# Three attention edits in one fused kernel: state reads in three float32r passes, conversions of w_out moved to the third stage, and token chunks of 368, 368 and 352 columns

## The chip, the cores and the metric

The kernel runs on one core of a Trainium2 chip, in one launch. The time is that of the device in microseconds. Three runs of the kernel before gave 825.01, 826.60 and 826.59 us, so the median is 826.59 us. The engines are named as in the profile: PE (TensorE matmul), PEld (its weight loads), DVE (VectorE), ACT (ScalarE), POOL (GpSimd) and SP, which issues the DMAs.

## The reference

The input is `x` of 4 x 8 heads x 512 tokens x 64 and a small `state` of 32 tokens for each head. Attention goes both ways and gives 4 x (512 + 32) = 2176 rows of 512 features, on which two MLPs follow.

```python
scores = scale * x @ state.T;  a = softmax(scores);   xread = a @ state
scores2 = scale * state @ x.T; a2 = softmax(scores2); sread = a2 @ x
x = concat([xread, sread])                  # tokens x 512
h = x @ w_in                                # 512 -> 2048
g = where(h >= 1, h, where(h <= -1, 0, (h + 1) ** 2 / 4))
y = g @ w_out                               # 2048 -> 512
out = ((y @ w_a) * (y @ w_b)) @ w_out2      # 512 -> 1536 -> 512
```

The weights of both MLPs arrive as float64; the kernel turns them into float32 itself. The matmuls of the MLPs are done in float32r: each float32 operand is split into a high part that float32r holds exactly and the rest, and three passes (high x high, high x low, low x high) make one product.

## The kernel before

There are four stages. In the first, attention is worked through in 8 quads (4 heads of one batch each), and at the same time the first product `x @ w_in` runs in tiles of 128 features x one token block; the blocks are 512, 512, 512, 320 and 320 tokens, so there are 80 tiles (`h_mm`, 12 matmuls each). Each tile's `g` is stored to DRAM. In the second stage (`b_chunk`) the product `g @ w_out` is made by a seven-product scheme (Strassen's, in Winograd's form) that halves tokens and features; in the third (`ab_run`) `y @ w_a` and `y @ w_b` are made in the same way. Both of these go over the tokens in three chunks. `CH` gives a chunk's columns and where its two halves start, so one chunk of 362 columns stands for 2 x 362 tokens, and the three together for 2176. The fourth stage (`o_group`) makes the last product.

Names that the change touches. `a_load` fetches a quad's `x` (`xld`) and state (`st`); `a_qk` makes the scores; `a_soft` the softmax down to `at`, the transposed weights; `a_read` reads the state, `st.T @ at`, in two matmuls of plain float32, one for the partitions 0 to 63 and one for 64 to 127, each into a PSUM bank of its own (6 and 7 in turn), and splits the result into the high and low parts of `x`. `s_soft`, `s_tr` and `s_read` are the other direction. `split` makes the two parts of an operand (one ACT and one DVE instruction). `conv` turns float64 words into float32: two loads, one ACT and four DVE instructions. `u_conv` is new. `w_put` and `w_sums` prepare the weights of the third stage in it.

The order of the work is not that of the code. Every operation is recorded with what it reads and writes (`Flow.op`), and `Flow.order` then plays a list schedule: each engine takes the ready operation with the earliest due time, with costs that are written into the code. Only the matmuls that are not `loose` keep the order of the code. The attention matmuls are `loose`, so a change in their costs or dependencies moves instructions on all engines. Each engine then runs its list strictly in order.

Of the kernel before, what the change touches and what calls it, by code (L numbers as in the profile page):

```python
# [20 lines left out]
class Flow:  # L21
# [16 lines left out]
    def op(self, engs, emit, rd=(), wr=(), size=0, loose=False):  # L38
        i = len(self.ops)
        if loose:  # L40
            self.loose.add(i)
        deps = set()
        last, readers = self.last, self.readers

        def cells(regs):
            for space, lo, hi in regs:
                g = self.GRAIN[space[0]]
                for c in range(lo // g, -(-hi // g)):
                    yield space, c
# [12 lines left out]
        self.ops.append((engs, emit, sorted(deps), size))  # L62
        return i
# [97 lines left out]
def attention_then_two_mlps(  # L161
# [13 lines left out]
    nc = tc.nc  # L175
    P = 128
    NQ = xt_d.shape[0]
# [7 lines left out]
    OFF = [sum(BLK[:j]) for j in range(len(BLK))]  # L185
    NB = len(BLK)

    CH = [(362, 0, 362), (362, 724, 1086), (364, 1448, 1812)]
    PAD = 368
    SCALE = 0.125  # L190
    WARM = 11


    QUAD = 8 * PAD * 4
# [28 lines left out]
    class V2:  # L223
# [17 lines left out]
        @property  # L241
        def regs(self):
            a = BASE[self.arena] + self.at
            return [("S", a + 4 * self.step * i, a + 4 * (self.step * i + self.n)) for i in range(self.k)]
# [17 lines left out]
    def bank(b):  # L262
        return ("P", b, b + 1)

    def dram(name, row, a, b):
        return ("D" + name, row * 4096 + a, row * 4096 + b)
# [27 lines left out]
    def store(dst, src, wr, size):  # L294
        op({"SP": 0.06}, lambda e: nc.sync.dma_start(out=dst(), in_=src()), regs(src), wr, size)
# [170 lines left out]
    def a_soft(k):  # L466
        d = qs[k]
        t1, b = d["t1"], sbank[k]
        mx, sm = d["sm"].sub(16, 16), d["sm"].sub(32, 16)
        op({"DVE": 0.72}, lambda e: nc.vector.transpose(t1(), banks[b]), [bank(b)], regs(t1))  # L470
        op({"DVE": 0.69}, lambda e: nc.vector.reduce_max(mx(), g32(t1()), axis=AX.X), regs(t1), regs(mx))
        op(
            {"POOL": 1.35},
            lambda e: eng(e).tensor_tensor(g32(t1()), g32(t1()), b32(mx()), ALU.subtract),
            regs(t1, mx),
            regs(t1),
        )
        act(t1, t1, 512, AF.Exp, regs(t1), regs(t1), scale=SCALE)
        op({"DVE": 0.69}, lambda e: nc.vector.reduce_sum(sm(), g32(t1()), axis=AX.X), regs(t1), regs(sm))
        op({"DVE": 0.25}, lambda e: nc.vector.tensor_scalar(sm(), sm(), 1e-9, None, ALU.add), regs(sm), regs(sm))  # L480
        op({"DVE": 0.25}, lambda e: nc.vector.reciprocal(sm(), sm()), regs(sm), regs(sm))
        op(
            {"POOL": 1.35},
            lambda e: eng(e).tensor_tensor(g32(t1()), g32(t1()), b32(sm()), ALU.mult),
            regs(t1, sm),
            regs(t1),
        )
        op({"DVE": 0.71}, lambda e: nc.vector.transpose(d["at"](), t1()), regs(t1), regs(d["at"]))

    def a_read(k):  # L490
        d = qs[k]
        b, q = divmod(k, 2)
        for p in range(2):
            ab = abank()
            r = slice(64 * p, 64 * p + 64)

            def emit(e, ab=ab, r=r):
                nc.tensor.matmul(banks[ab], d["st"]()[r, 128:], d["at"]()[r, :], start=True, stop=True)  # L498

            op({"PE": 0.9}, emit, regs(d["st"], d["at"]), [bank(ab)], loose=True)  # L500
            m = 2 * q + p
            for j, o, c, n in x_parts(b * S, S):
                hi, lo = (x[j][i].sub(m * BLK[j] + o, n) for i in range(2))
                src = lambda ab=ab, c=c, n=n: banks[ab][:, c : c + n]
                hi_of(hi, src, n, [bank(ab)], regs(hi))
                tt(lo, src, lambda hi=hi: hi(F32), ALU.subtract, n, [bank(ab)] + regs(hi), regs(lo))
# [292 lines left out]
    def x2_chunk(c, at):  # L799
        n, t0, t1 = CH[c]  # L800
        q = [V2(at[0], at[1] + 2944 * i, 2, PAD, n) for i in range(4)]
        for v, (r, tok) in zip(q, ((0, t0), (0, t1), (2, t0), (2, t1))):
            load(
                v,
                lambda r=r, tok=tok: x2_d[r : r + 2, :, tok : tok + n].rearrange("k p n -> p k n"),
                [dram("X", r + i, tok, tok + n) for i in range(2)],
                1024 * n,
            )
        b11, b12, b21, b22 = q

# [12 lines left out]
        v_sum(b21, b21, b22, ALU.subtract)  # L823
        sp("4", b21)
# [161 lines left out]
    def phase_one():  # L986
        a_load(0)
        a_load(1)
        for k in range(2):
            w_in(k, 1)  # L990
            a_qk(k)
            a_soft(k)
        warm(WARM)
        a_read(0)
        a_read(1)
        nv = nw = 0
        for t, (j, f) in enumerate((j, f) for j in range(NB) for f in range(F1)):
            if j == 0 and f % 2 == 0 and f + 2 < F1:
                w_in(f + 2, 2)
            h_mm(j, f)  # L1000

            if t in (0, 2, 8, 12, 17, 21, 25, 29):
                k = (0, 2, 8, 12, 17, 21, 25, 29).index(t)
                s_soft(k)
                s_tr(k)
                s_read(k)
                if k + 2 < NQ:
                    a_load(k + 2)
                    a_qk(k + 2)
                    a_soft(k + 2)  # L1010
                    a_read(k + 2)
            if 28 <= t < 60 and t % 4 == 0:
                conv([w1_d[2 * (nv + i) + 1] for i in range(2)], stage_a(), V("F0", vraw[nv].at, 1024))
                nv += 2
            if 34 <= t < 66 and t % 4 == 2:

                d = w32_a()
                ks = (F2 + nw, F2 + nw + 1) if nw < 4 else (nw - 4, nw - 3)
                conv([w2_d[3 * (k % F2 % 2) + k % F2 // 2 if k >= F2 else 3 * k + 2] for k in ks], stage_a(), d)
                for i, k in enumerate(ks):  # L1020
                    store(lambda k=k: u_d[k], d.sub(512 * i, 512), [dram("U", k, 0, 512)], 1 << 18)
                nw += 2
        assert (nv, nw) == (F1, F2 + 4)

    stage_l = Ring([V("F1", 2 * QUAD - 3584, 2048)])
    stage_c = Ring([V("F0", 11776 + 8192 * i, 2048) for i in range(2)])
# [15 lines left out]
    for c in range(3):  # L1042
        b_chunk(c, late if c == 2 else lambda k: None)
    x2_chunk(2, ("F0", VRAW))
    for fp in range(F2 // 2):
        for c in range(3):
            more = fp + 1 < F2 // 2
            s = 2 * fp + 2

            def done_a(c=c, s=s, more=more):  # L1050
                if c == 2 and more:
                    w_put(s + 1, combs[1 + s % 2])

# [77 lines left out]
```

## Time and profile before

| | before |
|---|---|
| median of 3 runs | 826.59 us (825.01 to 826.60) |
| profiled execution, whole time | 824.32 us |
| profiled execution, span of the instructions | 822.5 us |
| PE busy | 800.4 us (97%) |
| DVE / ACT busy | 570.7 us (69%) / 397.4 us (48%) |
| mean granted TensorE clock | 0.991 |

The span is 1.8 us shorter than the profiled execution's own time; the rest lies around it. The stages by the trace: the first 24 us are a start in which PE mostly waits; the first stage's tiles run to 255 us, the second stage to 423, the third to 679, the fourth to the end. Busy times of PE are made of records whose ends are modelled and which overlap, so the pace of PE is read from the number of matmuls in a stretch, not from its busy share.

### The profile page before, as it was taken

To read this page: it belongs to the slowest core of one execution; us is meant where nothing else is said; L and a number is where in the kernel's file an instruction comes from. 1 tells how busy PE (TensorE), PEld (TensorE's weight loads), DVE (VectorE), ACT (ScalarE), POOL (GpSimd) and SP (SyncE) were. 2 spreads that over 40 slices of the span, in tenths; PEclk is the share of its full clock that TensorE was granted. 3 is DMA by queue.
4 is the path that set the end of the run, shared out by engine and by line. 5 is a ranking of instruction groups with operands and counts; after the bars stand their busy time and mean duration, and the time that the engine had idled before them with its cause. 6 is when DMAs were issued, how large, how long until landed. Compare 5 with 4: busy or idle time off the path is not lost.

```text
span 822.5 us, 11669 instructions
## 1 busy us (share of the span) xinstructions
PE 800.4 (97%) x4338; PEld 727.2 (88%) x4338; DVE 570.7 (69%) x847; ACT 397.4 (48%) x655; POOL 21.6 (3%) x22
## 2 busy tenths in 40 slices
PE   4999999999999999999999999999999999999997
PEld 2766667889999999999999999999999998888886
DVE  6999998888567886886989998858464674322100
ACT  2777657656587444445665444343423563222100
POOL 2001120000000000000000000000000000000000
PEclk8899999999999999999999999999999999999999
DMA  8676686787634671270543344413142466433101
GB/s 300 207 272 213 200 290 242 277 281 260 229 118 136 218 234 50 81 224 19 157 146 109 119 143 154 153 48 134 50 163 71 142 191 215 142 102 100 68 0 65
DMA packets 71865, 130.01 MB, mean 158 GB/s; under 512 B 7168, under 2 KB 41472, under 8 KB 71808
## 3 DMA queue, kind: packets, MB, share of 16 engines
q1 hardware_dynamic: 71808, 129.27, 47.3%
q8 instruction: 34, 0.56, 0.3%
q14 instruction: 23, 0.19, 0.1%
HBM read 84.93 MB, written 44.30 MB: 157 GB/s over the span
## 4 chain that ended last, share of the span: by engine, by line
PE 86%; DVE 8%; DMA 2%; issue 2%; ACT 1%; SPq 1%; DVEq 0%; ACTq 0%
PE bank L328 82%; DMA f<-in_w_dram 2%; PE bank L498 1%; DVE f L379 1%; PE bank L563 1%; DVE f L371 1%; DVE f L313 1%; DVE r L313 1%; DVE f L357 1%; DVE f L612 1%; DMA g_d<-f 1%; ACT f L304 1%; SPq L292 0%; DVE f L363 0%; PE bank L454 0%
## 5 line engine op out<-in xcount | busy, mean ns | idle before, releaser
L328 PE MATMUL bank<-r 128*128 128x512 f32 (+3 forms) x3084 | 596.6, 351 | 3.1 <-DVE r L313 1.6
L328 PEld LDWEIGHTS bank<-r 128*128 128x128 f32 x3084 | 531.1, 188 | 61.5 <-issue 8.6
L313 DVE TENSOR_TENSOR r<-f,r 128x512 fp32r<-128x512 f32 (+5 forms) x224 | 190.8, 864 | 109.3 <-ACT r L304 103.7
L304 ACT ACTIVATE r<-f 128x512 fp32r<-128x512 f32 (+5 forms) x224 | 170.1, 771 | 171.6 <-PE bank L328 154.3
L328 PE MATMUL bank<-r,r 128*128 128x362 f32 (+1 forms) x1008 | 178.4, 329 | 1.6 <-DVE f L313 1.1
L328 PEld LDWEIGHTS bank<-r,r 128*128 128x128 f32 x1008 | 169.1, 189 | 2.8 <-DVE f L313 2.1
L304 ACT ACTIVATE f<-bank 128x362 f32<-128x362 f32 (+2 forms) x167 | 80.5, 485 | 162.6 <-PE bank L328 161.1
L313 DVE TENSOR_TENSOR f<-bank,f 128x362 f32<-128x362 f32 (+1 forms) x144 | 75.6, 532 | 61.2 <-PE bank L328 52.2
L304 ACT ACTIVATE f<-f 128x512 f32<-128x512 f32 (+2 forms) x123 | 87.3, 724 | 25.9 <-DMA f<-in_w_dram 18.7
L313 DVE TENSOR_TENSOR f<-f 128x256 f32<-128x256 f32 (+5 forms) x110 | 83.1, 778 | 0.3
L605 ACT ACTIVATE f<-bank,half 128x512 f32<-128x512 f32 (+1 forms) x80 | 49.4, 622 | 42.7 <-PE bank L328 36.4
L612 DVE SCALAR_TENSOR_TENSOR f<-f,bank 128x512 f32<-128x512 f32 (+1 forms) x80 | 47.4, 602 | 17.9 <-ACT f L304 11.8
L371 DVE SCALAR_TENSOR_TENSOR f<-f 128x1024 uint32<-128x1024 uint32 (+1 forms) x35 | 43.0, 1230 | 0.3
L379 DVE SCALAR_TENSOR_TENSOR f<-f 128x1024 uint32<-128x1024 uint32 (+1 forms) x35 | 42.6, 1218 | 0.1
L357 DVE TENSOR_SCALAR f<-f 128x1024 f32<-128x1024 f32 (+1 forms) x35 | 25.6, 733 | 9.8 <-ACT f L304 9.2
L965 DVE COPY f<-bank 128x512 f32<-128x512 f32 x8 | 5.5, 692 | 28.1 <-PE bank L328 28.1
L498 PE MATMUL bank<-f 64*128 64x512 f32 x32 | 16.1, 765 | 8.9 <-DVE f L480 6.6
L363 DVE TENSOR_SCALAR f<-f 128x1024 uint32<-128x1024 uint32 (+1 forms) x35 | 24.1, 687 | 0.1
L313 DVE TENSOR_TENSOR f<-f,f 128x724 f32<-128x724 f32 (+1 forms) x24 | 21.6, 908 | 0.9 <-DMA f<-g_d 0.8
L304 ACT ACTIVATE r<-bank 64x64 fp32r<-64x64 f32 (+3 forms) x36 | 13.4, 378 | 16.6 <-PE bank L498 7.9
L498 PEld LDWEIGHTS bank<-f 64*128 64x128 f32 x32 | 4.6, 216 | 15.0 <-DVE f L480 7.4
L313 DVE TENSOR_TENSOR r<-bank,r 64x64 fp32r<-64x64 f32 (+3 forms) x36 | 14.6, 413 | 3.3 <-ACT r L304 3.0
(33 smaller groups left out, 130.1 us busy)
## 6 DMA issues: line engine op xcount, KB each, us to landing
f<-in_w_dram SPq DMA_DIRECT2D x68, 512.0 KB, 4.7
g_d<-f SPq DMA_DIRECT2D x48, 256.0 KB, 4.0
f<-p_d SPq DMA_DIRECT2D x48, 256.0 KB, 2.8
f<-g_d SPq DMA_DIRECT2D x32, 362.0 KB, 4.3
p_d<-f SPq DMA_DIRECT2D x48, 181.0 KB, 2.4
f<-g_d SPq DMA_DIRECT2D x16, 364.0 KB, 4.0
g_d<-f SPq DMA_DIRECT2D x32, 160.0 KB, 1.8
p_d<-f SPq DMA_DIRECT2D x24, 182.0 KB, 2.0
```

Of the source, the lines that this page charges most:

```text
L304: lambda e: nc.scalar.activation(dst(), src(), func, **{k: (v() if callable(v) else v) for k, v in kws.items()}),
L313: op({"DVE": t_tt(n)}, lambda e: nc.vector.tensor_tensor(dst(), a(), b(), alu), rd, wr)
L328: nc.tensor.matmul(o, w, x, start=first and k == 0, stop=last and k == n - 1, skip_group_check=onto)
L357: lambda e: nc.vector.tensor_scalar(dst(), dst(), LEAST, MOST, ALU.max, ALU.min),
L363: lambda e: nc.vector.tensor_scalar(dst(U32), dst(U32), 3, 0x3FFFFFFF, ALU.logical_shift_left, ALU.bitwise_and),
L371: lambda e: nc.vector.scalar_tensor_tensor(dst(U32), word(1, U32)(), 0xC0000000, dst(U32), ALU.bitwise_and, ALU.bitwise_or),
L379: lambda e: nc.vector.scalar_tensor_tensor(dst(U32), word(0, U32)(), 29, dst(U32), ALU.logical_shift_right, ALU.bitwise_or),
L498: nc.tensor.matmul(banks[ab], d["st"]()[r, 128:], d["at"]()[r, :], start=True, stop=True)
L563: nc.tensor.matmul(banks[ab][:, p * 64 : (p + 1) * 64], d["xn"]()[:, c * 256 + p * 128 : c * 256 + (p + 1) * 128], d["a2t"]()[:, c * 128 + ...
L605: lambda e: nc.scalar.activation(q(), h(), AF.Relu, bias=half[:, 0:1], scale=0.5),
L612: lambda e: nc.vector.scalar_tensor_tensor(g(), q(), 1.0, h(), ALU.min, ALU.max),
L965: op({"DVE": t_tt(512)}, lambda e, o=o, b=b: nc.vector.tensor_copy(o(), banks[b]), [bank(b)], regs(o))
```

## The change

There are three edits. First, in quads 4 to 7 the state read is made in three float32r passes: the state's 128 columns and `at` are split into two parts each (`s3`, `w3`), and one operation issues six matmuls, the two partition halves alternating, into both banks. Quads 0 to 3 keep the two float32 matmuls. A further branch for the scores (`x3`) is written for quads from 99 on, of which there are none. Second, the third weight matrix of the second MLP (`w_out2`, 12 blocks, `u_d`) was converted in the first stage, two blocks at a time; now it is converted block by block in the third stage (`u_conv`). In the first stage two conversions for the first blocks of `w_a` and `w_b` are left. Third, the chunks have 368, 368 and 352 columns in place of 362, 362 and 364.

```diff
-    CH = [(362, 0, 362), (362, 724, 1086), (364, 1448, 1812)]
+    CH = [(368, 0, 368), (368, 736, 1104), (352, 1472, 1824)]
...
+    for k in range(4, NQ):
+        o = (XAT[4] + 10240, XAT[2] + 16384)[k % 2]
+        qs[k]["w3"] = [V("R0", o + 2048 * i, 512) for i in range(2)]
+        qs[k]["s3"] = [V("R0", o + 4096 + 512 * i, 128) for i in range(2)]
...
     def a_qk(k):
+        if "w3" in d:
+            split(*d["s3"], d["st"].sub(128, 128))
...
         op({"DVE": 0.71}, lambda e: nc.vector.transpose(d["at"](), t1()), regs(t1), regs(d["at"]))
+        if "w3" in d:
+            split(*d["w3"], d["at"])
 
     def a_read(k):
         d = qs[k]
         b, q = divmod(k, 2)
+        abs_ = [abank() for _ in range(2)]
+        if "w3" in d:
+
+            def emit3(e):
+                for i, (w, x) in enumerate(three(d["s3"], d["w3"])):
+                    for p in range(2):
+                        r = slice(64 * p, 64 * p + 64)
+                        nc.tensor.matmul(banks[abs_[p]], w()[r, :], x()[r, :], start=i == 0, stop=i == 2)
+
+            op({"PE": 0.75}, emit3, regs(*d["s3"], *d["w3"]), [bank(ab) for ab in abs_], loose=True)
         for p in range(2):
-            ab = abank()
+            ab = abs_[p]
...
-            op({"PE": 0.9}, emit, regs(d["st"], d["at"]), [bank(ab)], loose=True)
+            if "w3" not in d:
+                op({"PE": 0.9}, emit, regs(d["st"], d["at"]), [bank(ab)], loose=True)
...
-            if 34 <= t < 66 and t % 4 == 2:
+            if t in (62, 66):
 
                 d = w32_a()
-                ks = (F2 + nw, F2 + nw + 1) if nw < 4 else (nw - 4, nw - 3)
-                conv([w2_d[3 * (k % F2 % 2) + k % F2 // 2 if k >= F2 else 3 * k + 2] for k in ks], stage_a(), d)
...
+                conv([w2_d[3 * i + nw // 2] for i in range(2)], stage_a(), d)
...
+    def u_conv():
+
+        k, d = nu[0], V("F0", 36352, 512)
+        conv([w2_d[3 * k + 2]], stage_c(), d)
+        store(lambda: u_d[k], d, [dram("U", k, 0, 512)], 1 << 18)
+        nu[0] += 1
+
     for fp in range(F2 // 2):
         for c in range(3):
...
+            if fp and nu[0] < F2:
+                u_conv()
```

What this does to the order is read at three places. The first is PE's list in the first stage around the read of quad 4 (L498 before; L529 is the new read, L537 the old one in the new file; L454 and L481 are the scores, L328 and L329 the tiles of `h_mm`, L549 and L589 the transposes, L563 and L603 the `s_read`). Before:

```order
L563 MATMUL bank_74<-f_89 128x64 x8
L454 MATMUL bank_72<-f_66 64x512 x2
L328 MATMUL bank_68<-r_65 128x512 x12
L498 MATMUL bank_73<-f_89 128x512
L498 MATMUL bank_74<-f_89 128x512
L328 MATMUL bank_69<-r_65 128x512 x12
```

And now:

```order
L329 MATMUL bank_67<-r_65 128x512 x12
L481 MATMUL bank_72<-f_66 64x512 x2
L603 MATMUL bank_74<-f_89 128x64 x8
L481 MATMUL bank_71<-f_89 64x512 x2
L329 MATMUL bank_68<-r_65 128x512 x12
L529 MATMUL bank_73<-r_65 128x512
L529 MATMUL bank_74<-r_65 128x512
```

The last two rows come three times in a row. The scores of quad 6 (bank_71) now stand before the read of quad 4, where they stood after it, and the scores of quad 5 (bank_72) before the `s_read`.

The second place is SP's list, where the states of quads 4 to 7 are fetched (`in_st`; f_89 is the buffer of even quads, f_66 that of odd ones). Before, each fetch waited for the read of the quad two before it:

```order
L292 DMA f_66<-in_st_dram 128x256
L295 DMA g_d<-f_89 128x512
L292 DMA f_89<-in_xn_dram 128x1024
L295 DMA g_d<-f_89 128x512
L292 DMA f_66<-in_xt_dram 128x512 x2
L292 DMA f_66<-in_w_dram 128x1024 x2
L292 DMA f_89<-in_st_dram 128x256
```

Now quad 6's fetch waits for the split of quad 4's state alone, and stands just ahead of quad 5's:

```order
L293 DMA f_89<-in_st_dram 128x256
L293 DMA f_66<-in_st_dram 128x256
L296 DMA g_d<-f_89 128x512
L293 DMA f_66<-in_xt_dram 128x512 x2
L293 DMA f_66<-in_st_dram 128x256
L296 DMA g_d<-f_89 128x512
```

The fetches of quads 6, 5 and 7 (in this order) are now close together, and the weights' fetch is behind them.

The third place is DVE's list at the end of the first stage, where the tiles become 320 tokens wide (L612 and L652 make `g` and free the tile's bank; L357, L363 and L371 belong to a conversion). Before:

```order
L612 SCALAR_TENSOR_TENSOR f_89<-f_89,bank_69 128x320
L313 TENSOR_TENSOR r_65<-f_89,r_65 128x2x362
L357 TENSOR_SCALAR f_66<-f_66 128x1024
L363 TENSOR_SCALAR f_66<-f_66 128x1024
L371 SCALAR_TENSOR_TENSOR f_66<-f_66 128x1024
L612 SCALAR_TENSOR_TENSOR f_89<-f_66,bank_70 128x320
```

And now:

```order
L652 SCALAR_TENSOR_TENSOR f_89<-f_89,bank_67 128x320
L314 TENSOR_TENSOR r_65<-f_89,r_65 128x736
L652 SCALAR_TENSOR_TENSOR f_89<-f_66,bank_68 128x320
L652 SCALAR_TENSOR_TENSOR f_89<-f_89,bank_69 128x320
L652 SCALAR_TENSOR_TENSOR f_89<-f_66,bank_70 128x320
```

The conversions between the bank releases are gone from there.

## Rows read from the trace of the kernel before

**Rows 1.** Page, part 1: busy us (share of the span) xinstructions.

```profile
PE 800.4 (97%) x4338; PEld 727.2 (88%) x4338; DVE 570.7 (69%) x847; ACT 397.4 (48%) x655; POOL 21.6 (3%) x22
```

**Rows 2.** Busy by stretch: us, PE (x), PEld, DVE, ACT, POOL, clock, DMA, GB/s.

```profile
24.00:200.00 176.00, 173.26 (x805) 132.92 (x804) 158.33 (x245) 120.10 (x198) 16.41 (x12) 0.99 0.73 251
200.00:255.00 55.00, 53.66 (x364) 53.13 (x364) 35.37 (x53) 38.62 (x72) 0.00 (x0) 1.00 0.50 170
255.00:367.00 112.00, 112.00 (x672) 111.61 (x671) 91.12 (x115) 55.62 (x76) 0.00 (x0) 1.00 0.53 163
367.00:423.00 56.00, 56.00 (x337) 55.80 (x336) 45.72 (x56) 32.53 (x46) 0.00 (x0) 1.00 0.31 102
423.00:476.00 53.00, 51.35 (x304) 50.15 (x303) 49.38 (x73) 29.97 (x49) 0.00 (x0) 1.00 0.38 121
476.00:679.00 203.00, 202.25 (x1214) 201.95 (x1213) 142.49 (x225) 84.22 (x153) 0.00 (x0) 1.00 0.37 125
```

**Rows 3.** Waits of PE: who it waited for, us in total, times, longest.

```profile
PE bank L328 <- DVE r L313: 2.1, 3, 0.8
PE bank L549 <- DVE r L313: 1.2, 1, 1.2
PE bank L328 <- DVE f L612: 1.2, 1, 1.2
PE bank L328 <- DVE f L313: 1.1, 2, 0.7
```

**Rows 4.** As rows 2, stretches of one width: 320, 362, 364, 512 columns.

```profile
225.00:250.00 25.00, 25.00 (x171) 25.00 (x172) 17.00 (x25) 21.05 (x39) 0.00 (x0) 1.00 0.34 114
260.00:360.00 100.00, 100.00 (x601) 99.74 (x599) 81.33 (x105) 48.11 (x66) 0.00 (x0) 1.00 0.51 158
370.00:420.00 50.00, 50.00 (x301) 49.80 (x300) 40.71 (x49) 29.59 (x41) 0.00 (x0) 1.00 0.33 107
700.00:800.00 100.00, 100.00 (x443) 82.84 (x442) 21.80 (x39) 20.29 (x39) 0.00 (x0) 1.00 0.27 85
```

**Rows 5.** PE's timeline: start us, us, instructions; reads of quads 4, 6, 7.

```profile
92.17 1.25 PE L498 MATMUL bank<-f 64*128 64x512 f32 x4
...
118.21 1.13 PE L498 MATMUL bank<-f 64*128 64x512 f32 x4
119.27 5.76 PE L328 MATMUL bank<-r 128*128 128x512 f32 x24
...
129.89 1.12 PE L498 MATMUL bank<-f 64*128 64x512 f32 x2
130.95 3.01 PE L328 MATMUL bank<-r 128*128 128x512 f32 x12
133.89 1.12 PE L498 MATMUL bank<-f 64*128 64x512 f32 x2
```

**Rows 6.** Splits of 128x512, 476 to 679 us: busy us, mean ns | idle before.

```profile
L313 DVE TENSOR_TENSOR r<-f,r 128x512 fp32r<-128x512 f32 x35 | 23.0, 683 | 0.0
L304 ACT ACTIVATE r<-f 128x512 fp32r<-128x512 f32 x37 | 21.9, 626 | 5.5 <-PE bank L328 5.2 <-DVE f L379 0.2
```

**Rows 7.** As rows 2, the stretch of the reads of quads 4 to 6.

```profile
84.00:118.00 34.00, 32.63 (x159) 22.86 (x158) 32.02 (x56) 20.63 (x38) 6.89 (x5) 1.00 0.66 230
```

**Rows 8.** DMA issues: KB each, median us to landing.

```profile
f<-in_st_dram SPq DMA_DIRECT2D x8, 128.0 KB, 2.8
```

**Rows 9.** DVE's instructions of a conversion, 24 to 200 us.

```profile
L379 DVE SCALAR_TENSOR_TENSOR f<-f 128x1024 uint32<-128x1024 uint32 x21 | 26.7, 1272 | 0.1
L371 DVE SCALAR_TENSOR_TENSOR f<-f 128x1024 uint32<-128x1024 uint32 x21 | 26.3, 1252 | 0.2
L357 DVE TENSOR_SCALAR f<-f 128x1024 f32<-128x1024 f32 x21 | 16.3, 776 | 6.9 <-ACT f L304 6.5
L363 DVE TENSOR_SCALAR f<-f 128x1024 uint32<-128x1024 uint32 x21 | 14.6, 694 | 0.1
```

**Rows 10.** Timeline around 207 us, the conversion before PE's wait for L612.

```profile
207.32 0.69 DVE L357 TENSOR_SCALAR f<-f 128x1024 f32<-128x1024 f32 x1 [2.72 <-ACT f L304]
```

**Rows 11.** Waits of DVE from 476 to 679 us.

```profile
DVE f L313 <- PE bank L328: 47.5, 53, 2.5
```

More of the change, by code (lines that the diff above doesn't have):

```diff
@@ L191, in attention_then_two_mlps @@
     WARM = 11
+    STEPS = (0, 2, 8, 12, 17, 21, 25, 29)
     QUAD = 8 * PAD * 4
@@ L427, in attention_then_two_mlps @@
     qs = [{**sets[k % 2], "a2": a2s[k % 2], "sm": sms[k % 4]} for k in range(NQ)]
+    for k in range(4, NQ):
+        o = (XAT[4] + 10240, XAT[2] + 16384)[k % 2]
+        qs[k]["w3"] = [V("R0", o + 2048 * i, 512) for i in range(2)]
+        qs[k]["s3"] = [V("R0", o + 4096 + 512 * i, 128) for i in range(2)]
+        if k >= 99:
+            qs[k]["x3"] = [V("R0", XAT[1] + 8192 * (k % 2) + 4096 * i, 1024) for i in range(2)]
+            qs[k]["q3"] = [V("R0", o + 5120 + 512 * i, 128) for i in range(2)]
     sbank = [4 + k % 2 for k in range(NQ)]
@@ L449, in a_qk @@
         b = sbank[k]
+        if "w3" in d:
+            split(*d["s3"], d["st"].sub(128, 128))
+        if "x3" in d:
+            for i in range(2):
+                split(*(v.sub(512 * i, 512) for v in d["x3"]), d["xld"].sub(512 * i, 512))
+            split(*d["q3"], d["st"].sub(0, 128))
+            def emit3(e):
+                for k, (w, x) in enumerate(three(d["q3"], d["x3"])):
+                    for p in range(2):
+                        r = slice(64 * p, 64 * p + 64)
+                        nc.tensor.matmul(
+                            banks[b][r, :], w()[:, r], x()[:, p * 512 : (p + 1) * 512], start=k == 0, stop=k == 2
+                        )
+            op({"PE": 0.72}, emit3, regs(*d["q3"], *d["x3"]), [bank(b)], loose=True)
+            return
         def emit(e):
@@ L492, in a_read, with emit3 @@
         b, q = divmod(k, 2)
+        abs_ = [abank() for _ in range(2)]
+        if "w3" in d:
+            def emit3(e):
+                for i, (w, x) in enumerate(three(d["s3"], d["w3"])):
+                    for p in range(2):
+                        r = slice(64 * p, 64 * p + 64)
+                        nc.tensor.matmul(banks[abs_[p]], w()[r, :], x()[r, :], start=i == 0, stop=i == 2)
+            op({"PE": 0.75}, emit3, regs(*d["s3"], *d["w3"]), [bank(ab) for ab in abs_], loose=True)
         for p in range(2):
-            ab = abank()
+            ab = abs_[p]
             r = slice(64 * p, 64 * p + 64)
@@ L1000, in phase_one @@
             h_mm(j, f)
-            if t in (0, 2, 8, 12, 17, 21, 25, 29):
-                k = (0, 2, 8, 12, 17, 21, 25, 29).index(t)
+            if t in STEPS:
+                k = STEPS.index(t)
                 s_soft(k)
@@ L1014, in phase_one @@
                 nv += 2
-            if 34 <= t < 66 and t % 4 == 2:
+            if t in (62, 66):
                 d = w32_a()
-                ks = (F2 + nw, F2 + nw + 1) if nw < 4 else (nw - 4, nw - 3)
-                conv([w2_d[3 * (k % F2 % 2) + k % F2 // 2 if k >= F2 else 3 * k + 2] for k in ks], stage_a(), d)
-                for i, k in enumerate(ks):
-                    store(lambda k=k: u_d[k], d.sub(512 * i, 512), [dram("U", k, 0, 512)], 1 << 18)
+                conv([w2_d[3 * i + nw // 2] for i in range(2)], stage_a(), d)
+                for i in range(2):
+                    store(lambda k=F2 + nw + i: u_d[k], d.sub(512 * i, 512), [dram("U", F2 + nw + i, 0, 512)], 1 << 18)
                 nw += 2
-        assert (nv, nw) == (F1, F2 + 4)
+        assert (nv, nw) == (F1, 4)
     stage_l = Ring([V("F1", 2 * QUAD - 3584, 2048)])
@@ L1044, in attention_then_two_mlps @@
     x2_chunk(2, ("F0", VRAW))
+    nu = [0]
+    def u_conv():
[3 more added lines that the diff above has]
+        nu[0] += 1
     for fp in range(F2 // 2):
```

## The prediction

> **What bounds the kernel now.** I read the engines' busy time first, then the same by stretch, then PE's waits. PE is busy 97% of the span, DVE 69% [rows 1]. By stretch PE is busy nearly without a break from 24 us to the end of the third stage, at a granted clock of 0.99 to 1.00 [rows 2], and the waits that the profile gives it after its start come to 5.6 us: 2.1 + 1.2 + 1.2 + 1.1 [rows 3]. So from 24 us on whatever PE no longer has to do is time, unless a wait takes its place. The engine from which such a wait would come is DVE: it is busy 158 of 176 us in the first stage (90%), 32.0 of 34 us (94%) where quads 4 to 6 are read [rows 7], and 49.4 of 53 us (93%) at the start of the third stage. Behind that it has room: 142 of 203 us (70%) [rows 2].
>
> PE's pace is read from counts of matmuls. A stretch counts about one matmul more than it issues, since one is in flight at its edge. So 320 columns take 25 us / 170.5 = 146.7 ns, 512 take 100 / 441.2 = 226.7, 362 take 100 / 600 = 166.7 and 364 take 50 / 300 = 166.7 [rows 4]. The line through 320 and 512 rises by 80.0 / 192 = 0.4167 ns per column. On it 362 columns would take 164.2 ns and 364 take 165.0, and both rows lie above, at what the line gives for 368. So 362 and 364 are charged as 368, as if columns were rounded up to a multiple of 8 or 16. This is what the third edit rests on.
>
> **The chunks.** A chunk has 2 x 168 = 336 matmuls in the second stage (56.0 us by the 337 counted from 367 to 423 us [rows 2]: 56.0 / 336 = 166.7) and 504 in the third (6 pairs of blocks x 2 matrices x 42). The first two chunks go to 368 columns, which are charged already: no change. The third goes to 352 = 22 x 16, which the line puts at 146.7 + 32 x 0.4167 = 160.0 ns, 6.7 ns less than now. That is 336 x 6.67 = 2.24 us in the second stage and 504 x 6.67 = 3.36 us in the third, 5.6 us in all. Not all of it need arrive: at 423 to 476 us DVE is 93% busy and PE waits 53.0 - 51.35 = 1.65 us there [rows 2]. If PE comes there 2.2 us sooner and DVE's own list shortens by about 1 us (its instructions on the third chunk are 3% shorter), PE waits 1.2 us more. I take -5.6 + 1.2 = -4.4. The bounds are 0 (the pace is linear in columns, whose total does not change) and -5.6.
>
> A rule of the Trainium skill speaks against this edit. "TensorE: Matmul & The Clock Gate", section Back-to-back issue gap, gives columns / 2.4 + 2.5 ns per matmul. That is 153.3 ns at 362 columns against the row's 166.7, and it has no rounding: by it the edit gives nothing and the sum below is 4.4 us smaller. The row is on the other side, so I follow the row.
>
> **The reads of quads 4 to 7.** A float32 read of one half takes 1.06 us (129.89 to 130.95), and two halves side by side take the same 1.06 us together (118.21 to 119.27, four records): halves of different partitions overlap [rows 5]. Before, quads 4 and 6 are read side by side (1.17 and 1.06), quads 5 and 7 half by half (2 x 1.05 each, quad 7's at 129.89 and 133.89): 6.4 us. Each switch between the kinds costs too: the 12 matmuls between quad 7's halves take 133.89 - 130.95 = 2.94 us against 12 x 0.2267 = 2.72, so 0.2 us per block, and six blocks become four. Now a quad has three passes of 512 columns at 226.7 ns. If the halves overlap as they do in float32, this is 0.68 us per quad and 2.7 us in all; if not, six passes make 1.36 and 5.4 us. So the term is 6.4 - 2.7 + 2 x 0.2 = -4.1 us, or at the other bound 6.4 - 5.4 + 0.4 = -1.4. I take -4.1, since the rows of quads 4 and 6 show the overlap.
>
> What it adds is two splits per quad. That of `at` is 626 ns on ACT and then 683 ns on DVE [rows 6]; that of the state, a quarter as long, lies between nothing and that. Both halves of the read wait for them, and so do the banks' next users. In PE's new list the scores of quad 5 stand before the `s_read`, and so nearer to the fetch of quad 5's state, which has 2.8 us to landing [rows 8] and now stands on SP behind quad 6's fetch, which waits for DVE's split. Behind a late fetch SP holds g stores, and DVE holds the releases of the tile banks. DVE has only 2 us in 34 free here [rows 7]. Bounds: nothing, where the tile's 2.7 us between them cover it, and 4 x (0.63 + 0.68) + 0.4 = 5.6 us, where each quad's split and one fetch are bare. In this stretch PE already waits once for 1.2 us (L549 [rows 3]), a wait that the old order made. I expect two or three of such a size and take +1.0 us net.
>
> **The moved conversions.** Six conversions of two blocks leave the first stage, each with 1.27 + 1.25 + 0.78 + 0.69 = 4.0 us of DVE [rows 9]: 24 us of DVE, 12 loads and 12 stores. PE is the bound there, so this is worth what PE's waits for DVE were worth behind the attention. One of these goes: at 207.32 a conversion that had waited 2.72 us for ACT [rows 10] stands ahead of L612 in DVE's list, and PE waits 1.2 us for the tile bank [rows 3]. In the new order there are bank releases alone at that place. I take -1.3 us, with 0 and -1.3 as bounds. In the third stage there come 12 conversions of one block, half as long: between 12 x 2.0 = 24 us of DVE and, if a half costs as much as a whole, 48. Its waits for PE alone are 47.5 us [rows 11], so the first fits twice over and I price it at nothing. If the cover is gone, it is a rival below. Nothing else reaches the start up to 24 us, whose DVE and PE lists are the same, nor the fourth stage.
>
> **Sum.** -4.4 (chunks) - 4.1 (reads) + 1.0 (new waits) - 1.3 (conversions out of the way) = -8.8 us against the profiled execution's 824.32 us (span 822.5 and 1.8 around it): 815.5. The median of the runs lies 2.3 us above that execution, so as a median it is 826.59 - 8.8 = 817.8 us. With the bounds the likeliest case reaches from 826.59 - 5.6 - 4.1 - 1.3 = 815.6 (no new wait), less the runs' own spread of 1.6 us, to some 820.5 (the reads' halves not overlapped).
>
> **Rivals.**
> 1. The first stage takes the reads' gain back: the splits and the late fetches are bare, +5.6 in place of +1.0. Then 817.8 + 4.6 = 822.4 us. For it speaks DVE at 94% [rows 7]; against it, that 24 us of conversions can be put off to where DVE is freer. Chance 0.15.
> 2. The pace is linear in columns, the excess of 362 and 364 over the line has another cause that stays, and the chunks give 0: 817.8 + 4.4 = 822.2 us. Equal paces of 362 and 364 speak against it [rows 4]. Chance 0.06. The rule of the Trainium skill above is of this kind.
> 3. Slower: DVE's list in the third stage. A conversion's four instructions stand in order ahead of bank releases that PE needs, and the two staging buffers are shared with the weights' conversions, so that `w_put` comes late. Each of the 12 conversions can hold PE up by its 2.0 us of DVE: +24 us, 841.8. It decides from 8.8 / 12 = 0.73 us per conversion, which makes no change; at half its price it is 829.8 us. Against it: no wait of PE for weights is listed there now, and 47.5 us of DVE's waits are for PE [rows 11]. Chance 0.04.
>
> The likeliest case has 0.75. The range of 814.0 to 822.4 takes in its own (814.0 to 820.5) and most of rivals 1 and 2; outside lies rival 3 and the worse part of 1. A difference of less than 0.2% (1.65 us) cannot be told from none. Faster than 824.94 us: 0.75 + 0.14 + 0.04 = 0.93; slower than 828.24: 0.03; the rest, 0.04, is the same.
>
> **What would show it.** A stretch of 352 columns should issue one matmul per 160.0 ns and one of 368 per 166.7; 163 or 153 would be wrong for the rounding. The reads of quads 4 to 7 should take about 0.7 us each in the timeline; 1.36 would mean no overlap. PE's wait for L652 near 207 us should be gone, and new waits should stand between 75 and 115 us, at the reads, the transposes behind them or the scores of quads 5 and 6, with 1 to 3 us in all. PE's waits at the start of the third stage should grow by about 1 us, and DVE's busy time from there to the fourth stage by 24 us or more with no wait of PE after it. What would make the time wrong is a wait of PE in the third stage behind a conversion, or more than 5 us of waits in the first.

## The result, and the profile after

| | before | after |
|---|---|---|
| median of 6 runs each, side by side | 825.51 us (824.38 to 826.60) | 814.61 us (814.34 to 818.09) |
| ratio | | 0.9874, 95% interval 0.9855 to 0.9893 |
| the same pair again, later (11 and 6 runs) | 824.87 us | 815.19 us, ratio 0.9880 (0.9860 to 0.9900) |
| profiled execution (span) | 824.32 us (822.5) | 814.35 us (812.6) |

The change makes the kernel 1.2 to 1.3% faster. 817.8 us was predicted, with a range of 814.0 to 822.4.

Where the 9.97 us of span come from is read from the start of the first matmul of each part (the first record of its tiles in each trace):

| part | before, us | after, us | difference |
|---|---|---|---|
| up to the first tile | 24.5 | 24.3 | -0.2 |
| 48 tiles of 512 columns, attention between them | 172.2 | 167.4 | -4.8 |
| 32 tiles of 320 columns | 58.2 | 56.3 | -1.9 |
| second stage, chunks 1, 2 and 3 | 56.2, 56.1, 56.2 | 57.0, 56.5, 53.8 | -1.1 |
| third stage | 255.7 | 253.7 | -2.0 |
| fourth stage | 143.4 | 143.4 | 0 |

Busy time of the changed kernel, and the same by stretch, in the columns of [rows 1, 2]. PE is busy 7 us less in all. From 24 to 200 us it is busy 1.5 us more, since it waits less there.

```profile
PE 793.1 (98%) x4346; PEld 723.3 (89%) x4346; DVE 575.0 (71%) x879; ACT 401.4 (49%) x669; POOL 22.6 (3%) x22
```

```profile
24.00:200.00 176.00, 174.80 (x847) 137.95 (x846) 150.91 (x242) 122.45 (x209) 17.40 (x12) 0.99 0.67 225
200.00:255.00 55.00, 55.00 (x371) 55.00 (x370) 29.81 (x44) 38.26 (x70) 0.00 (x0) 1.00 0.30 100
255.00:367.00 112.00, 111.61 (x666) 111.12 (x665) 89.96 (x114) 54.15 (x75) 0.00 (x0) 1.00 0.51 158
367.00:423.00 56.00, 56.00 (x350) 55.77 (x349) 48.13 (x60) 35.19 (x51) 0.00 (x0) 1.00 0.36 118
423.00:476.00 53.00, 51.27 (x304) 49.88 (x304) 50.21 (x77) 25.91 (x45) 0.00 (x0) 1.00 0.33 110
476.00:679.00 203.00, 202.24 (x1210) 200.21 (x1209) 164.10 (x271) 92.77 (x165) 0.00 (x0) 1.00 0.55 183
```

The waits of PE behind its start follow. The two of 1.2 us in [rows 3], for the transposes (L549 before) and for L612, are gone, and none of that size has come.

```profile
PE bank L329 <- DVE r L314: 2.1, 3, 0.8
PE bank L329 <- DVE f L314: 1.4, 3, 0.8
PE bank L537 <- DVE r L314: 0.4, 1, 0.4
```

PE's timeline at the reads of quads 4, 5 and 7, which answers to [rows 5] (start, length of the group, instructions; L529 is the new read, L589 the transposes):

```profile
93.09 0.97 PE L529 MATMUL bank<-r 64*128 64x512 f32 x6
93.99 3.02 PE L329 MATMUL bank<-r 128*128 128x512 f32 x12
96.84 0.60 PE L589 MATMUL bank<-ident,f 128*128 128x128 f32 x4
...
105.87 0.96 PE L529 MATMUL bank<-r 64*128 64x512 f32 x6
106.76 5.73 PE L329 MATMUL bank<-r 128*128 128x512 f32 x24
...
137.22 0.96 PE L529 MATMUL bank<-r 64*128 64x512 f32 x6
138.11 2.10 PE L329 MATMUL bank<-r 128*128 128x512 f32 x8
```

Each read takes 0.90 us (93.09 to 93.99). Its six matmuls start in pairs 4 ns apart (93.090 and 93.094, 93.425 and 93.429, 93.660 and 93.664), so the halves do overlap. The transposes at 96.84 have no wait before them. DVE is as full here as before, and PE has no gap (columns of [rows 7], then the stretch of the old wait for L612):

```profile
84.00:118.00 34.00, 34.00 (x177) 25.63 (x176) 32.38 (x67) 24.43 (x51) 10.36 (x7) 1.00 0.61 201
195.00:226.00 31.00, 31.00 (x213) 31.00 (x213) 13.38 (x23) 20.84 (x41) 0.00 (x0) 1.00 0.33 119
```

DVE's waits from 476 to 679 us, which answer to [rows 11]. DVE is busy 164.1 - 142.5 = 21.6 us more there, which are the moved conversions, and its waits for PE fell by 22.2. (The third stage ends at 669 us now, so the last 10 us of this stretch belong to the fourth; experiment 3 has both stretches alike.)

```profile
DVE f L314 <- PE bank L329: 25.3, 42, 1.5
DVE r L314 <- ACT r L305: 5.9, 7, 1.7
DVE f L358 <- ACT f L305: 2.0, 2, 1.8
```

### The profile page after: what moved, and what is told of

It reads as the page before. It is cut to its first block, busy times and chain, and to the rows that moved or that the text cites. A ratio compares the mean times of both kernels' runs of the same rounds, so it can differ in the third digit from the quotient of the medians.

```text
span 812.6 us, 11751 instructions
## 1 busy us (share of the span) xinstructions
PE 793.1 (98%) x4346; PEld 723.3 (89%) x4346; DVE 575.0 (71%) x879; ACT 401.4 (49%) x669; POOL 22.6 (3%) x22
## 4 chain that ended last, share of the span: by engine, by line
PE 89%; DVE 6%; DMA 2%; issue 1%; ACT 1%; SPq 0%; DVEq 0%; ACTq 0%
PE bank L329 85%; DMA f<-in_w_dram 2%; PE bank L603 2%; DVE f L380 1%; DVE f L372 1%; DVE f L314 1%; PE bank L537 1%; DVE r L314 1%; DVE f L358 1%; ACT r L305 1%; PE bank L481 0%; PE bank L529 0%; PE bank L589 0%; SPq L293 0%; DVE f L652 0%
## 5 line engine op out<-in xcount | busy, mean ns | idle before, releaser
L329 PE MATMUL bank<-r 128*128 128x512 f32 (+3 forms) x3084 | 594.2, 350 | 2.0 <-DVE r L314 1.6
L329 PEld LDWEIGHTS bank<-r 128*128 128x128 f32 x3084 | 528.8, 188 | 57.7 <-issue 7.0
L314 DVE TENSOR_TENSOR r<-f,r 128x512 fp32r<-128x512 f32 (+4 forms) x232 | 194.9, 851 | 108.3 <-ACT r L305 102.5
L305 ACT ACTIVATE r<-f 128x512 fp32r<-128x512 f32 (+5 forms) x232 | 174.0, 760 | 172.2 <-PE bank L329 147.0
L329 PE MATMUL bank<-r,r 128*128 128x368 f32 (+1 forms) x1008 | 177.1, 328 | 1.7 <-DVE f L314 1.1
L329 PEld LDWEIGHTS bank<-r,r 128*128 128x128 f32 x1008 | 167.5, 188 | 3.1 <-DVE f L314 2.1
L305 ACT ACTIVATE f<-bank 128x368 f32<-128x368 f32 (+2 forms) x167 | 80.2, 484 | 149.6 <-PE bank L329 147.4
L314 DVE TENSOR_TENSOR f<-bank,f 128x368 f32<-128x368 f32 (+1 forms) x144 | 75.2, 533 | 34.8 <-PE bank L329 29.8
L652 DVE SCALAR_TENSOR_TENSOR f<-f,bank 128x512 f32<-128x512 f32 (+1 forms) x80 | 47.9, 604 | 32.7 <-ACT f L305 31.6
L314 DVE TENSOR_TENSOR f<-f,f 128x736 f32<-128x736 f32 (+1 forms) x24 | 21.6, 909 | 0.7 <-DMA f<-g_d 0.7
L537 PE MATMUL bank<-f 64*128 64x512 f32 x16 | 9.2, 889 | 8.9 <-DVE f L507 6.5
L603 PEld LDWEIGHTS bank<-f 128*128 128x128 f32 x128 | 15.4, 191 | 1.4 <-ACT f L645 0.8
```

The lines of the kernel that those rows point to most:

```text
L305: lambda e: nc.scalar.activation(dst(), src(), func, **{k: (v() if callable(v) else v) for k, v in kws.items()}),
L314: op({"DVE": t_tt(n)}, lambda e: nc.vector.tensor_tensor(dst(), a(), b(), alu), rd, wr)
L329: nc.tensor.matmul(o, w, x, start=first and k == 0, stop=last and k == n - 1, skip_group_check=onto)
L603: nc.tensor.matmul(banks[ab][:, p * 64 : (p + 1) * 64], d["xn"]()[:, c * 256 + p * 128 : c * 256 + (p + 1) * 128], d["a2t"]()[:, c * 128 + ...
L652: lambda e: nc.vector.scalar_tensor_tensor(g(), q(), 1.0, h(), ALU.min, ALU.max),
```

## The experiments

Ratios are to the kernel before, run beside each. It took 825.73 us beside `e1_chunks` to `e4_pair4`, 826.02 beside `e5_w384`, `e6_w356`, `e8_all3` and `e9_copy`, and 824.87 beside the rest.

**1. The chunks alone** (`e1_chunks`: the kernel before with one line changed).

```diff
-    CH = [(362, 0, 362), (362, 724, 1086), (364, 1448, 1812)]
+    CH = [(368, 0, 368), (368, 736, 1104), (352, 1472, 1824)]
```

> The kernel before with the chunks of 368, 368 and 352 columns alone. Theory A (columns are charged in steps, and 368 pays 1.1 ns more than 362 does): 1680 x 1.1 ns lost, 840 x 6.8 ns won, a new wait of 0.6 us in the second stage: 3 us faster, and the stretch to 255 us as before. Theory B (the prediction's sum, 368 as dear as 362): 4.4 to 5.6 us faster. Theory C (pace linear in columns): no change.

822.91 us, ratio 0.9968 (0.9950 to 0.9986): -2.8 us. The prediction's -4.4 was too much. In this run's trace the second and third stages are 3.1 us shorter, but the first is 1.4 us longer: its new order has two waits for L612, 2.3 us in all, where one of 1.2 stood. The count of matmuls shows why the chunks give less than 4.4 (PE's matmuls of the chunks alone; columns: us, PE busy (x), clock, DMA share, GB/s). First the kernel before, then the changed one; 305 to 360 us lies in the first two chunks, 368 to 412 in the third:

```profile
305.00:360.00 55.00, 55.00 (x332) 1.00 0.39 118
368.00:412.00 44.00, 44.00 (x266) 1.00 0.30 95
```

```profile
305.00:360.00 55.00, 55.00 (x329) 1.00 0.39 115
368.00:412.00 44.00, 44.00 (x277) 1.00 0.37 122
```

55 us hold three matmuls fewer at 368 columns than at 362, and 44 us eleven more at 352 than at 364. From start to start, over all neighbours of one width in the second stage, 362 takes 166.66 ns, 364 166.65, 352 159.56 and 368 167.79.

**2. The reads alone** (`e2_reads`: the three-pass reads of the change in the kernel before, old conversions and chunks).

> The kernel before with the three-pass reads of quads 4 to 7 alone; conversions and chunks as before. Theory A (PE's time for the reads is what counts): 3.2 us faster, up to 4.8 if the waits near 96 and 112 us go with the old order. Theory B (the reads pay only because the conversions make room on DVE): new waits of 1 to 3 us between 75 and 115 us, so 0 to 2 us faster.

821.34 us, ratio 0.9939 (0.9914 to 0.9964): -4.4 us, as the first theory has it. The place of the gain is plain. From the start of the 17th tile to that of the first tile of 320 columns, where quads 4 to 7 are read, it takes 113.2 us before, 112.8 with the conversions alone (experiment 3), and 108.5 both here and in the changed kernel. The wait for the transposes went with the reads; with the conversions alone it stays (1.3 us). With the old conversions around the reads, the wait for L652 (L612 before) remains, and one for ACT is there ahead of the 17th tile:

```profile
PE bank L329 <- ACT r L305: 1.7, 1, 1.7
PE bank L329 <- DVE f L652: 1.3, 2, 1.1
```

**3. The conversions alone** (`e3_convs`: only the six calls of `conv` for `w_out2` moved to `u_conv`).

> The kernel before with the conversions of w_out in the third stage alone. Theory A: PE's waits near 209 and 224 us go, 1.9 us faster, and up to 3.4 if those near 96 and 112 us go too. Theory B (PE was the bound, the conversions hid behind it): within 0.5 us of before. In the third stage neither expects a wait of PE behind a conversion; a third theory, that the conversions hold up bank releases there, expects over 1 us of new waits after 476 us.

823.60 us, ratio 0.9970 (0.9952 to 0.9989): -2.1 us. The tiles of 320 columns lost the 1.9 us that they lost in the whole change, and the third stage took 255.7 us as before. The profiled execution's span is only 0.1 us shorter (822.4), since the new order put a wait for ACT into the first stage (PE's timeline, first fence below). The stretch from 476 us shows DVE 22.5 us fuller with PE as busy as in [rows 2]:

```profile
58.16 0.73 PE L329 MATMUL bank<-r 128*128 128x512 f32 x2 [2.09 <-ACT r L305]
```

```profile
200.00:255.00 55.00, 55.00 (x377) 55.00 (x376) 28.82 (x45) 38.67 (x75) 0.00 (x0) 1.00 0.27 95
476.00:679.00 203.00, 202.26 (x1214) 201.95 (x1214) 164.99 (x273) 91.50 (x164) 0.00 (x0) 1.00 0.52 172
```

The three parts alone give -2.8 - 4.4 - 2.1 = -9.3 us, together -9.7 to -10.9: they add up within the error.

**4. What in the reads is worth the time.** `e4_pair4` is the changed kernel with quads 4 to 7 read in float32, both halves in one operation, and without the splits.

```diff
...
+        if k >= 4:
+
+            def emit2(e):
+                for p in range(2):
+                    r = slice(64 * p, 64 * p + 64)
+                    nc.tensor.matmul(banks[abs_[p]], d["st"]()[r, 128:], d["at"]()[r, :], start=True, stop=True)
+
+            op({"PE": 1.1}, emit2, regs(d["st"], d["at"]), [bank(ab) for ab in abs_], loose=True)
...
```

> The changed kernel without its splits and passes: quads 4 to 7 are read in float32, but the two halves in one operation, side by side. Theory A (most of the reads' gain is that halves of quads 5 and 7 no longer stand apart): a read takes 1.06 us against 0.90, so 0.6 to 1.0 us slower than the changed kernel, 9 us faster than before. Theory B (the three passes are the gain): 3 us slower than the changed kernel, 7 us faster than before.

817.89 us, ratio 0.9907 (0.9877 to 0.9936): 3.3 us slower than the changed kernel by the medians, 2.2 to 2.7 by the ratios, not 0.6 to 1.0. The size is the second theory's, but its reason is not: a read takes 1.06 us (92.36 to 93.42), so the passes themselves give only 4 x 0.16 = 0.64 us. In the traces the spans differ by 3.2 us, and most of the rest are waits: two of 1.1 and 0.8 us, and 0.5 us ahead of the 17th tile. PE's timeline (L530 is the read here, L474 the scores, L590 the transposes, L604 the `s_read`):

```profile
92.36 1.13 PE L530 MATMUL bank<-f 64*128 64x512 f32 x4
93.42 5.75 PE L329 MATMUL bank<-r 128*128 128x512 f32 x24
99.01 0.60 PE L590 MATMUL bank<-ident,f 128*128 128x128 f32 x4
100.71 1.08 PE L474 MATMUL bank<-f 128*64 128x512 f32 x4 [1.11 <-issue]
102.64 2.00 PE L604 MATMUL bank<-f 128*128 128x64 f32 x16 [0.84 <-ACT f L305]
```

The scores at 100.71 need the state of quad 6, which SP fetches into the buffer of quad 4's state. The float32 read holds that buffer until 93.5 us; then SP issues two fetches of weights, and the state's goes out at 95.36 and lands 5.3 us later, at 100.6. A split lets the buffer go early: in the changed kernel the same fetch is the first of two (of quads 6 and 5) at 81.45, with no fetch of weights just ahead of it. The second wait is for ACT, which had itself waited 2.52 us for weights. SP and ACT in `e4_pair4`, then SP in the changed kernel:

```profile
93.89 1.37 SPq L293 DMA_DIRECT2D f<-in_w_dram  x2
95.36 0.38 SPq L293 DMA_DIRECT2D f<-in_st_dram  x1
100.36 1.16 ACT L305 ACTIVATE f<-f 128x1024 f32<-128x1024 f32 x1 [2.52 <-DMA f<-in_w_dram]
```

```profile
81.45 1.81 SPq L293 DMA_DIRECT2D f<-in_st_dram  x2
```

**5. The buffer or the order?** Two runs on that. `e9_copy` is `e4_pair4` with the right half of the state copied by DVE first and read from the copy; `e14_pair4c` is `e4_pair4` with another cost for the planner, and so another order of the same instructions.

```diff
...
+        if k >= 4:
+            sc = V("F0", 59904 + 512 * (k % 2), 128)
+            d["sc"] = sc
+            op({"DVE": 0.2}, lambda e: nc.vector.tensor_copy(sc(), d["st"].sub(128, 128)()), regs(d["st"]), regs(sc))
...
```

```diff
-            op({"PE": 1.1}, emit2, regs(d["st"], d["at"]), [bank(ab) for ab in abs_], loose=True)
+            op({"PE": 0.75}, emit2, regs(d["st"], d["at"]), [bank(ab) for ab in abs_], loose=True)
```

> As e4_pair4 (reads of quads 4 to 7 in float32, both halves in one operation), with the right half of the state copied by DVE at the quad's start and read from the copy, so that the state's buffer is free for the fetch two quads on before the read. A, e4's loss of 3.3 us against the changed kernel is mostly the buffer held by a float32 read, which makes the scores and reads after it late: the waits at 100.7 (1.1) and 102.6 (0.8) go, and 0.64 us of pace and the splits' place remain: 815.2 to 815.8 us, ratio 0.987 to 0.988. B, the order that the planner makes of the other costs gives the waits, not the buffer: 817 to 818.5 us, ratio 0.990 to 0.991.

> e4_pair4 with the planner's cost of the four paired float32 reads at 0.75 in place of 1.1, as the three passes are costed; the instructions are the same, the order differs. A, e4's loss against the changed kernel is mostly its order: the waits at 100.7 and 102.6 us go, the passes' 0.64 us and at most 0.7 us of the state's buffer remain: 815.2 to 816 us, ratio 0.987 to 0.988. B, the loss belongs to float32 reads whatever the order: 817 to 818.5 us, ratio 0.990 to 0.991.

With the copy, quad 6's fetch goes out at 79.47 us and both waits are gone; the only new wait of `e9_copy` from 86 us on is 0.77 us at a read. But the copy also moved the order: the scores of quads 5 and 6 (L478, 8 matmuls) now stand together ahead of the read of quad 4 (L534). In `e14_pair4c` the waits stay. Its PE list around them came out as in `e4_pair4`, though, so it does not test the order there. SP and PE in `e9_copy` (L608 is the `s_read`), then in `e14_pair4c`:

```profile
79.47 0.37 SPq L293 DMA_DIRECT2D f<-in_st_dram  x1
...
87.88 1.94 PE L478 MATMUL bank<-f 128*64 128x512 f32 x8
90.58 1.38 PE L534 MATMUL bank<-f,f 64*128 64x512 f32 x4 [0.77 <-DVE f L512]
...
97.98 1.89 PE L608 MATMUL bank<-f 128*128 128x64 f32 x16
```

```profile
96.19 0.38 SPq L293 DMA_DIRECT2D f<-in_st_dram  x1
...
101.62 1.08 PE L474 MATMUL bank<-f 128*64 128x512 f32 x4 [1.18 <-issue]
103.52 2.00 PE L604 MATMUL bank<-f 128*128 128x64 f32 x16 [0.82 <-ACT f L305]
```

In the profiled executions this is worth what the buffer's theory says: over the stretch of experiment 2, from the 17th tile on, `e9_copy` takes 109.6 us, `e4_pair4` and `e14_pair4c` 111.3 each, and the changed kernel 108.5; the spans are 813.5, 815.8, 816.7 and 812.6 us. The medians do not bear it out: `e9_copy` has 817.32 us, ratio 0.9903 (0.9886 to 0.9919), which lies in its second theory's range and 0.6 us below `e4_pair4`, and its profiled execution of 815.29 was its shortest of four; `e14_pair4c` has 818.48, ratio 0.9926 (0.9899 to 0.9953). So the traces show that the two waits go where the buffer is released early and the planner makes an order of that. Which of the two does it, and how much of the 3.3 us it is worth in a usual run, stays open.

**6. More of the same?** `e8_all3` reads quads 2 and 3 in three passes too; `e11_best` (on `e5_w384` below) reads them in float32, both halves in one operation, with the `emit2` above for quads 2 and 3.

```diff
-    for k in range(4, NQ):
+    for k in range(2, NQ):
```

> The changed kernel with the reads of quads 2 and 3 in three passes too. A, the reads' gain holds for them: both stand apart in the changed kernel (2 x 1.25 us each), 1.10 each is left, 1.4 a quad: 2.8 us less, 811.8 us, ratio 0.983. B, quads 2 and 3 come where DVE is at its fullest (first tiles), their eight splits (some 4 us of DVE and ACT) bring waits of PE at 40 to 80 us as long as the gain: 814 to 816 us, ratio 0.986 to 0.989. C, slower than after by over 1 us.

> e5_w384 with the reads of quads 2 and 3 in float32 but both halves in one operation (no splits). A, the pairing gains there as it did for the quads 5 and 7 (1.4 us each where the halves stood apart): 2.8 us less than e5_w384, 811.2 us, ratio 0.982. B, the planner's new order of the first stage brings waits that eat it, as in e8_all3: 813 to 817 us, ratio 0.985 to 0.989.

Neither gained: `e8_all3` has 817.48 us, ratio 0.9896 (0.9878 to 0.9915), and a span of 815.8 us against the changed kernel's 812.6; `e11_best` has 816.26 us, ratio 0.9894 (0.9875 to 0.9913), and 815.5 us against the 811.2 of `e5_w384`. The 48 tiles of 512 columns with the attention between them took 170.9 and 171.5 us, against 167.4 in the changed kernel and 167.5 in `e5_w384`. The planner put out new orders, and PE waited in both. In `e8_all3`:

```profile
58.98 0.73 PE L329 MATMUL bank<-r 128*128 128x512 f32 x2 [2.02 <-ACT r L305]
67.36 2.56 PE L329 MATMUL bank<-r 128*128 128x512 f32 x10 [1.23 <-DVE r L314]
72.39 3.03 PE L329 MATMUL bank<-r 128*128 128x512 f32 x12 [1.02 <-DVE f L569]
```

`e11_best` adds no split and waited as much (6.6 us from 24 to 90 us in `e8_all3`, 6.8 in `e11_best`, 1.2 in the changed kernel), so it is not the splits' cost alone.

**7. What sets the pace of a chunk's matmul.** Three runs on widths and places. `e6_w356` has chunks of 366, 366 and 356. `e5_w384` has 352, 352 and 384, with buffer steps of 384 columns (1536 bytes) in the second stage and of the width itself in the third. `e10_stride` has 368, 368 and 352 in those same second-stage buffers, and the changed kernel's step in the third stage for 368. From the edit of `e5_w384`:

```diff
-    CH = [(368, 0, 368), (368, 736, 1104), (352, 1472, 1824)]
-    PAD = 368
+    CH = [(352, 0, 352), (352, 704, 1056), (384, 1408, 1792)]
+    PAD = 384
+    XB = [0, 112 * 352, 112 * 704]
...
-        return V2("R0", XC * c + 2944 * (2 * IDX[i] + h), 2, PAD, CH[c][0])
+        return V2("R0", XB[c] + 8 * CH[c][0] * (2 * IDX[i] + h), 2, CH[c][0], CH[c][0])
...
```

> The changed kernel with chunks of 366, 366 and 356 columns; a look at paces only. A, columns are rounded up to 16: 366 paces as 368 (167.8) and 356 as 368 too (166.7 to 167.8), no faster than before, 818 us or so. B, rounded up to 8: 366 as 368 (167.8), 356 as 360 (163.3): 1680 x 167.8 + 840 x 163.3 = 419.1 us, 3 more than after: 817.5 us. C, no rounding, (columns + 32) / 2.4: 366 at 165.8, 356 at 161.7 ns, as after.

> The changed kernel with chunks of 352, 352 and 384 columns (places of buffers shifted to fit). A, the pace is the columns plus 32 over 2.4 per ns and what 368 showed (167.8 in place of 166.7) belongs to 368: 352 takes 159.7, 384 takes 173.3 ns, so 1680 x 159.7 + 840 x 173.3 = 413.9 us against 1680 x 167.77 + 840 x 159.7 = 416.0: 2.1 less, 812.5 us, ratio 0.984. B, wide chunks above 362 to 364 all carry some 1.1 ns more: 384 takes 174.4, gain 1.2, 813.4 us, ratio 0.9855. C, the wide chunk last gives waits at the end of the second stage that eat it: 814.6 to 816 us, new waits of PE at 361 to 415 us.

> The changed kernel's chunks (368, 368, 352) with the second stage's operands at a step of 1536 bytes instead of 1472 (the buffers of e5_w384), the third stage's as in the changed kernel; a look at paces only. A, the pace of a matmul depends on where its moving operand starts: in the second stage 368 takes 166.7 and 352 takes 160.0 ns, each the same for all six positions, in the third stage 167.8 and 159.9 as before; second stage 1.0 us shorter in all (672 x 1.1 less 336 x 0.4, with the new wait left). B, the width alone sets it: 167.8 in both stages.

Mean ns from start to start of neighbours of one width:

| columns (step) | second stage | third stage |
|---|---|---|
| 352 (1472 bytes, after) | 159.56 | 159.85 |
| 352 (1536; 1408 in the third, `e5_w384`) | 160.07 | 160.90 |
| 352 (1536; 1408 in the third, `e10_stride`) | 160.97 | 159.51 |
| 356 (1472, `e6_w356`) | 162.23 | 162.09 |
| 362, 364 (1472, before) | 166.66, 166.65 | 166.61, 166.58 |
| 366 (1472, `e6_w356`) | 168.87 | 168.31 |
| 368 (1472, after) | 167.79 | 167.79 |
| 368 (1536; 1472 in the third, `e10_stride`) | 166.71 | 167.86 |
| 384 (1536, `e5_w384`) | 173.42 | 173.39 |

The control is `e10_stride`: the same 368 columns take 166.71 ns where rows are 1536 bytes apart, 167.86 in its third stage where they are 1472 apart, and 167.79 in the same second stage of the changed kernel, 1472 apart. The granted clock is 1.00 in each stretch, and the count from 305 to 360 us is 331 in place of 329:

```profile
305.00:360.00 55.00, 55.00 (x331) 1.00 0.39 114
```

So the place of the operands moves the pace, and the 1.1 ns are not the width's. The first theory there was right on 368 and wrong on the rest: its six positions are not equal (164.6 to 168.9 ns in the first chunk), and 352 came out at 161.0, not 160.0. No rounding fits `e6_w356`: 356 lies near the prediction's line through 320 and 512 columns, which gives 161.7 ns, while 366 takes more than 368. It ran once, in 819.13 us. The step alone is not the rule either: 352 columns at 1408 bytes take 160.90 ns in one kernel and 159.51 in the other. What rule joins place and width stays open; single steps between 154 and 177 ns repeat by position in the list.

`e5_w384` has 813.97 us, ratio 0.9856 (0.9842 to 0.9871), and a span of 811.2 us against 812.6, the shortest of all. The gain on the changed kernel is that of its second stage, 166.4 us against 167.4, of which some 0.5 us is the wait in the first chunk that is gone, and 0.3 us in the third. Its counts, 352 and then 384 columns (the third chunk starts at 356 us, so the last 4 us of the first row have 384 columns):

```profile
305.00:360.00 55.00, 55.00 (x343) 1.00 0.40 123
368.00:412.00 44.00, 44.00 (x255) 1.00 0.37 120
```

The medians, 813.97 and 814.61 or 815.19 us, lie closer than the runs' spread, so the profile alone carries this.

**8. The changed kernel again** (`e12_after`), beside the last three.

> The changed kernel itself, on the same chip as the others of this call, so that they stand against it directly. 814.6 us, ratio 0.9868 to 0.9874; outside 0.9855 to 0.9893 the first result's size would be in doubt.

815.19 us, ratio 0.9880, as in the table at the top.

## Why the prediction was right

The forecast was the likeliest case, and three of its four terms had the right sign; the new waits did not. That the sum came within 1.2 us of the span's fall is in part luck: the waits were missed by 2.6 us and the conversions by 0.6 one way, the reads by 0.9 and the chunks by some 1.2 the other. The sizes, in its own steps:

- **The reads** were put at -4.1 us. A read takes 0.90 us in place of 0.68. The term's own working with that is 6.4 - 4 x 0.90 + 0.4 = 3.2 us less. The halves overlap, which was the choice between the bounds; the passes start 0.24 to 0.34 us apart, not 0.227. Most of the term is not the passes (0.64 us) but that quads 5 and 7 are no longer read half by half; this last is worked out from [rows 5], and no run has it alone.
- **The new waits** were put at +1.0 us, and this step failed. The prediction named DVE's splits and late fetches as the price of the reads; none of the waits between 75 and 115 us came. The wait of 1.2 us for the transposes went, and the 48 tiles lost 4.8 us against a reads' term of 3.2: -1.6 where +1.0 stood. The prediction saw that the fetch of a later state now waits for the split, and priced that as a delay. Against a float32 read, which holds the buffer longer, it comes sooner: quad 6's fetch went out at 81.45 us, where before it stood at 96.13, after the read of quad 4. What that is worth is as open as in experiment 5.
- **The conversions out of the way** were put at -1.3 us and gave -1.9: the wait for L612 and a smaller one behind it went. Alone they gave -2.1.
- **The moved conversions in the third stage** were put at nothing, and cost nothing: 21.6 us of DVE took the place of 22.2 us of its waits for PE, with PE's waits unchanged. With the conversions alone the third stage took 255.7 us, as before. So the slower rival falls.
- **The chunks** were put at -5.6, with 1.2 given back. The paces of 146.7 and 226.7 ns behind the line are right (from start to start 146.65 and 226.72), though the divisors 170.5 and 441.2 are not the rows' counts less one, as the text has it. 352 columns did about as said: (166.65 - 159.56) x 336 + (166.58 - 159.85) x 504 = 5.8 us. But 368 was not free: 672 x 1.13 + 1008 x 1.18 = 1.9 us. The 1.2 us at the start of the third stage did not come: PE is busy 51.27 us of 53 there against 51.35, and its waits in the whole stage are 2.4 us against 2.3. In its place there is one wait in the first chunk, with 0.6 us in all; PE's timeline:

```profile
289.84 6.71 PE L329 MATMUL bank<-r 128*128 128x368 f32 x39
296.94 3.25 PE L329 MATMUL bank<-r 128*128 128x368 f32 x18 [0.40 <-DVE f L314]
```

That is -5.8 + 1.9 + 0.6 = -3.3; the table of parts has -3.1, and the run alone -2.8. The argument that 362 and 364 cost the same and so stand for 368 was half right: the third chunk gave 7 ns a matmul and the two wider ones lost only 1.1, but equal means at two widths were no proof of a rounding. The rule of the Trainium skill that the prediction set against it ("TensorE: Matmul & The Clock Gate", section Back-to-back issue gap: columns / 2.4 + 2.5 ns) is stated there for a matmul by itself, which the prediction left out, and gives 149.2 ns at 352 columns; the trace, a stream of matmuls with a weight load each, has 159.6, so the rule does not hold for this stream.

- **The base.** The sum was -8.8 us against a span that fell by 9.97. The other 2.0 us of the miss lie in the 2.3 us between before's profiled execution and its median of three, which the prediction carried over; with three more runs of the kernel before the median of all six is 825.51, and the changed kernel's profiled execution lies 0.3 us below its median.

Rival 1, bare splits, falls by the 34 us at 84 to 118 us in which PE has no gap at all, with DVE at 32.4 us of them. Rival 2, a linear pace that gives nothing, falls by -2.8 us in experiment 1; why 362 and 364 columns lie above the line stays open.

## What to carry to other kernels

Where an operand is split or copied before it is used, count the buffer that the copy sets free, not the copy's work alone: here the next fetch into it went out some 14 us sooner (81.45 us against 95.36 with a float32 read). Equal paces at two widths don't show a rounding: measure the very width, at the very place in memory, before it is counted as free. Where a planner sets the order, a change of a stage's instructions or costs can bring several us of waits or take them away, so what one edit gained (quads 4 to 7) can't be carried over to the next (quads 2 and 3).

## What the runs showed that was not expected

A matmul over rows of 368 columns takes 166.71 ns where they lie 1536 bytes apart and 167.86 where they lie 1472 apart, in one kernel. Two float32r matmuls on different halves of the partitions start 4 ns apart and share their time, as two in float32 do; three such pairs took 0.90 us against 1.06 for one float32 pair. In the third stage 21.6 us more of DVE's work lengthened nothing.
